# A planner's cost model is rewritten: dependent neighbours, transfers, measured times, and four buffers for decoded tiles

## The chip, the cores and the metric

The kernel runs on one core of one Trainium2 chip. The metric is the device time of one execution in microseconds (us). The core has a matrix engine (TensorE, PE in the profile), a vector engine (VectorE, DVE), an activation engine (ScalarE, ACT), a general engine (GpSimd, POOL) and SyncE (SP), which here issues the transfers. Each engine runs its own queue in order; semaphores tie the queues together.

## The reference

Three parts are computed in sequence, for a batch of 4, all in float32.

- **Attention with decay.** 8 heads, 768 tokens, head size 48. With f = sigmoid(f_logit), a state of 48 x 48 per head is updated at every token, `state = f * state + outer(k, v)`, and `y = q @ state`. The heads are then joined to x of 768 x 384.
- **Block 1, a gated MLP.** `h = gelu_tanh(x @ w_in)` with 1024 columns, cut into u and v of 512. v is normalised over its 512 columns (mean, variance, eps 1e-6), multiplied by `g_ln`, mixed over tokens, `v_s = w_sg @ v_n + b_sg`, and `x = x + (u * v_s) @ w_out`.
- **Block 2, a mixing in the complex plane.** `theta = x @ w_theta`; `y = w_tok_r @ (x cos theta) + w_tok_i @ (x sin theta)`; `u = x + y`; the result is `u + relu(u @ w_ch)`.

The weights w_in, w_out, w_theta, w_ch, w_tok_r and w_tok_i come as float64, seen as pairs of 32-bit words; the kernel turns them into float32 itself (a "decode"). w_sg comes as float32.

## The kernel before, in words

**Matmuls in three parts.** Each float32 operand is split into a high part (a cast on ScalarE, `split` line 792, `xsplit` line 802, `load_split` line 446) and a low part (a subtraction on VectorE, lines 793, 803, 447). `mm3` (line 775) then multiplies high by high, high by low and low by high: lines 783, 784 and 785.

**Attention** (`half`, `unit`). The sequence is taken in two halves of 384 tokens, the heads in four pairs. A half loads the logits and q, k, v, makes decays with a scan on VectorE (line 562 for batch 0, line 578 else), and their logarithms and inverses on ScalarE (Ln and Exp, lines 583 and 584). A unit, one pair of one half, then runs on TensorE: transposes of k (628), updates (640) and scores (649), products inside a chunk (704) and products carried from earlier chunks (722). Between these ScalarE copies the transposed k (kt, 632), VectorE masks the scores (661) and sums the states (677 to 686) with ScalarE's scaling (691), and ScalarE copies y out (733). y goes by transfer into x's layout (`xst<-y`, 756). There are 32 units: 8 for each batch.

**Block 1** (`block1`): the v half of x @ w_in with gelu and statistics for six token tiles, p2 (u), p3 (token mixing; its PSUM is read on line 846), p4 (w_out). For batch b it is interleaved with the attention of batch b + 1. Per token tile, the sum of v comes from the gelu's accumulator (958), GpSimd multiplies it by -1/512 (963), ScalarE adds it (964) and squares with an accumulator (967); VectorE and GpSimd make the inverse root (974, 979).

**Block 2** (`block2`): theta with sine and cosine (888 to 898), p6 (token mixing with two weight matrices), p7 (w_ch). It runs for the last batch first and then for batches 0 to 2, whose x waits in DRAM.

**Weights.** The 24 tiles of w_tok_r and w_tok_i are decoded in the background (`decode`): load into `raw`, one ScalarE and four VectorE instructions into `dt` (432 to 436), the two parts into `wt`, a write to DRAM (`scratch<-wt`, 483). There is one `wt` buffer (`N_W = 1`). w_theta and w_ch are decoded into one buffer `wmid` of three tiles and written to DRAM in one transfer each (`channel_weights`). Streams read the tiles back (`st<-scratch`, 493) into five buffers.

**The order of the work.** The whole program is described as operations with an engine, a duration, the buffers read and written and a due time. `Plan.schedule` then simulates the engines in Python when the kernel is built and writes each engine's queue in the order that the simulation gives; nothing is reordered on the chip. It first moves due times back from successors. Then, for each engine, it takes the operations that could start within `LOOK` of the earliest one, and of these the one with the earliest due time, ScalarE's table switches being charged `SWITCH = 2.0`. Two operations on the same engine follow one another at once, by `lat`. A transfer is given an issue time, a rate and a landing time. PE's clock is modelled too, and while the plan is below 100 us, filler matmuls (line 1029) are put into TensorE's gaps.

Of the kernel before, what the change touches and what calls it, by code (L numbers as in the profile page):

```python
# [8 lines left out]
F32 = mybir.dt.float32  # L9
F32R = mybir.dt.float32r  # L10
# [38 lines left out]
WARM_GAP = 0.3  # L49
N_W = 1  # L50
N_DT = 3
# [59 lines left out]
class Op:  # L111
    __slots__ = ("eng", "dur", "fn", "deps", "succ", "left", "vt", "n", "start", "end", "need", "table", "dma", "est", "cols")


class Plan:
# [57 lines left out]
    def schedule(self):  # L173
        for o in reversed(self.ops):
            cost = LAT[o.eng] + o.dur + ((1.6 + o.dma / 360e3) * DMA_SLACK if o.dma else 0.0)
            for d in o.succ:
                o.vt = min(o.vt, d.vt - cost)
        free = {e: 0.0 for e in LAT}
        ticks = {}
        cand = {e: [] for e in LAT}  # L180
        table, dev, dge = None, 0.0, 0.0
        for o in self.ops:
# [49 lines left out]
        while todo:  # L232
            pick = None
            for e, c in cand.items():
                best = None
                ready = []
                for o in c:
                    t = o.est
                    if o.need:
                        u = slot_time(o)  # L240
                        if u is None:
                            continue
                        t = max(t, u)
# [80 lines left out]
def body(tc, ctx, att, qkv, flog, w_in, g_ln, w_sgT, b_sg, w_out, w_theta, w_rT, w_iT, w_ch, out):  # L324
# [42 lines left out]
    def make_state(attention):  # L367
# [6 lines left out]
        g.ar = [Slots(main, f"ar{i}_", 1) for i in range(3)]  # L374
        g.wmid = Slots(main, "wmid", 1)
        g.stat = Slots(main, "stat", 2)
# [23 lines left out]
    def dma(pl, eng, nbytes, fn, r=(), w=(), wp=(), vt=None):  # L400
        pl.op(eng, {"SP": 0.47, "ACT": 0.66, "POOL": 1.05}[eng], fn, r, w, wp, dma=nbytes, vt=vt)

# [6 lines left out]
    def a1(n):  # L409
        return 0.1 + n * 0.00081  # L410
# [50 lines left out]
    def channel_weights(pl, g, i, vt):  # L461

        w = pl.buf(g.wmid, [P, 2, NK, DM], F32R)
        src, scale = ((w_theta, 1.0 / (2.0 * math.pi)), (w_ch, None))[i]
        for k in range(NK):
            load_split(
                pl, g, w, lambda k=k: (w.t[:, 0, k], w.t[:, 1, k]), src[k * P : (k + 1) * P], vt + k * 2.0, scale, background=True
            )
        dma(pl, "SP", P * 9216, lambda: nc.sync.dma_start(scratch2[i], w.t.bitcast(F32)), [w], [g.scr2[i]], vt=vt + 6.0)

    def channel_load(pl, g, i, vt, place=None):

        w = pl.buf(g.wmid, [P, 2, NK, DM], F32R) if place is None else Buf(t=win[:, :, :, place * DM : (place + 1) * DM])
        old = [] if place is None else [x for xs_ in g.win for x in xs_]
        dma(pl, "SP", P * 9216, lambda: nc.sync.dma_start(w.t.bitcast(F32), scratch2[i]), [g.scr2[i]], [w, *old], vt=vt)
        return w
# [112 lines left out]
    def unit(pl, g, b, hf, p, f, fb, seed, sb, be, bb, t, parts, xst, carry):  # L589
# [42 lines left out]
        pl.op("ACT", a1(TH), lambda: nc.scalar.mul(kt.t, ps.t[:, 0, :TH], -1.0), r=[ps], w=[kt])  # L632
        nu = 2 * NC2 - hf
# [20 lines left out]
        here = Buf()  # L654
        pl.op("PE", 1.15, scores, r=[kb, qb, vb, kt], w=[ps, here])
        if before:
# [17 lines left out]
        def state(c):  # L674
            (s0, b0), (s1, b1) = S[c], S[c + 1]
            if hf == 0 and c == 0:
                pl.op("DVE", 0.2, lambda: V.tensor_copy(s1(), U(0)), r=[ps], w=[b1])
            elif c % 2 or c == 0:
                b1 = fulls[c // 2] if c % 2 else b1
                s1 = (lambda: st.t[:, 2 * NC2 + c // 2]) if c % 2 else s1  # L680
                pl.op("DVE", 0.16, lambda: V.tensor_add(s1(), s0(), U(c)), r=[ps, b0], w=[b1])  # L681
            else:
                be_ = be[:, c // 2 - 1 : c // 2]
                pl.op(
                    "DVE", 0.19,
                    lambda: V.scalar_tensor_tensor(s1(), st.t[:, 2 * NC2 + c // 2 - 1], be_, U(c), ALU.mult, ALU.add), r=[ps, fulls[c // 2 - 1], bb], w=[b1],
# [39 lines left out]

        carry["last"] = [qb, *(S[c][1] for c in late)], [ps], 0.15 * len(late), carried

        def output():
            y = pl.buf(g.y, [P, NC2, 2, HP])  # L730
            pl.op(
                "ACT", a1(TH),
                lambda: nc.scalar.copy(
# [36 lines left out]
    def moe(pl, g, xst, get, wmid, out_b, pace, first=False):  # L770
# [48 lines left out]
        def p2(hf):  # L819
            us = []  # L820
            for d in range(ND):
# [5 lines left out]
                u = pl.buf(g.u, [P, TH])  # L827
                pl.op("ACT", a1(TH), lambda u=u, ps=ps: A(u.t, ps.t[:, :TH], AF.Gelu_apprx_tanh), [ps], [u], table="G")  # L828
                us.append(u)
# [38 lines left out]
        def theta(hf, w):  # L868
            for i in range(NC2):
# [13 lines left out]

                pl.op("PE", 0.33, transposes, r=xst[hf].parts, w=[xps])
                pl.vt += 0.4 * pace
# [47 lines left out]
        def block1(before, resplit, keep=None):  # L933
# [10 lines left out]
            for s in range(NS):  # L944
# [7 lines left out]
                for k in range(NK):  # L952
# [8 lines left out]

                m = lambda s=s: stat.t[:, 0, s : s + 1]
                pl.op("POOL", 0.15, lambda m=m: nc.gpsimd.tensor_scalar(m(), m(), -1.0 / DH, None, ALU.mult), w=[sm[s]])
                pl.op("ACT", a1(DH), lambda m=m, vt=vt: A(vt.t, vt.t, AF.Identity, bias=m()), [sm[s]], [vt])  # L964
                pl.op(
                    "ACT", a1(DH) + 0.1,
                    lambda vt=vt, s=s: A(junk, vt.t, AF.Square, accum_out=stat.t[:, 1, s : s + 1]), [vt], [sv[s]],  # L967
                )
                vts.append(vt)
                if s % 3 == 2:  # L970
                    gs = slice(s - 2, s + 1)
                    pl.op(
                        "DVE", 0.07,
                        lambda gs=gs: V.tensor_scalar(stat.t[:, 2, gs], stat.t[:, 1, gs], 1.0 / DH, 1e-6, ALU.mult, ALU.add),
                        sv[gs], sr[gs],
# [56 lines left out]
    with tc.manual_schedule():  # L1032
        def between():
# [8 lines left out]
            pl.vt = U_AT  # L1042
            dma(pl, "SP", 2048, lambda: nc.sync.dma_start(gcol, g_ln), wp=[g.const])
            dma(pl, "SP", P * 3072, lambda: nc.sync.dma_start(bbc, b_sg.partition_broadcast(P)), wp=[g.const])
# [61 lines left out]
    def general():  # L1106
# [48 lines left out]
        with tc.For_i(0, B, 1) as b:  # L1155
# [4 lines left out]
            for hf in range(2):  # L1160
# [23 lines left out]
            one, two = moe(  # L1184
                pl, g, xin, lambda pl, i: stream(pl, g, i, 0.0), lambda pl, i: channel_load(pl, g, i, 0.0),
                out[bass.ds(b, 1)].squeeze(0), 1.0,
# [51 lines left out]
```

## Time and profile before

| | |
|---|---|
| median of 3 runs | 666.63 us (664.45 to 668.9) |
| profiled execution | span 668.6 us; highest of the three times 668.9 us |
| TensorE busy (matmul) | 616.4 us, 92% |
| TensorE weight loads | 568.9 us, 85% |
| VectorE busy | 445.6 us, 67% |
| ScalarE busy | 357.9 us, 54% |
| GpSimd busy | 30.0 us, 4% |
| transfers | 131.49 MB, mean 197 GB/s |

Busy times are the union of an engine's instructions over the span; a matmul's record is longer than the step to the next one, since they are pipelined. The page lists groups of instructions by source line and the chain of work that ended last. Block 1 of the last batch ends near 420 us; the rest of the span is block 2.

### The profile page before, as it was taken

The page shows a single profiled execution, that of the slowest core. Times are in us where ns is not written, and L with a number is a line of the kernel's source. Part 1 is how long each engine was busy: PE and PEld are TensorE (multiplying, and loading weights), DVE is VectorE, ACT ScalarE, POOL GpSimd, SP SyncE. Part 2 cuts the span into 40 slices and gives each one's busy share as a digit, 9 for nine tenths or more (in the row PEclk, how much of TensorE's full clock was granted, in tenths as well). Part 3 has the DMA queues.
Part 4 walks back from the last instruction along what each step waited for, and adds up shares of the span by engine and source line. Part 5 has one row for each costly group of instructions (what it writes and reads, how often), then busy time and mean ns, then how long its engine had stood idle before and what let it go on. Part 6 is the DMA issues. An engine that isn't in the chain of part 4 may idle for free.

```text
span 668.6 us, 14971 instructions
## 1 busy us (share of the span) xinstructions
PE 616.4 (92%) x5963; PEld 568.9 (85%) x5963; DVE 445.6 (67%) x1029; ACT 357.9 (54%) x754; POOL 30.0 (4%) x56
## 2 busy tenths in 40 slices
PE   9788699799999989899989999899999999999996
PEld 8677478687788877698878999899989999998996
DVE  6999689988879987758767488731581175148203
ACT  6759695667695557774337543730390065029200
POOL 2001010000200001200001000000000000000000
PEclk9999899899999999799989999999999999999999
DMA  8531846297456885444776678268628844860762
GB/s 327 207 93 52 308 159 212 90 311 247 161 156 221 296 286 178 137 134 151 227 251 221 213 278 295 73 193 254 203 78 279 249 161 145 255 214 25 250 198 76
DMA packets 54383, 131.49 MB, mean 197 GB/s; under 512 B 6816, under 2 KB 21664, under 8 KB 54048
## 3 DMA queue, kind: packets, MB, share of 16 engines
q1 hardware_dynamic: 54304, 130.45, 59.2%
q8 instruction: 49, 0.80, 0.5%
q14 instruction: 30, 0.25, 0.1%
HBM read 100.93 MB, written 24.77 MB: 188 GB/s over the span
## 4 chain that ended last, share of the span: by engine, by line
PE 45%; DVE 21%; ACT 17%; DMA 12%; issue 3%; POOL 1%; SPq 0%; POOLq 0%; DVEq 0%; ACTq 0%
PE mm L783 14%; PE mm L785 14%; PE mm L784 14%; DMA scratch<-wt 4%; DMA xst<-y 2%; DMA qkv<-in_qkv 2%; ACT junk L967 2%; ACT tmp L964 2%; DVE tmp L846 2%; DMA f<-in_flog 1%; ACT tmp L958 1%; DMA st<-scratch 1%; DVE s L681 1%; ACT ar L792 1%; DMA raw<-in_w_iT 1%
## 5 line engine op out<-in xcount | busy, mean ns | idle before, releaser
L783 PE MATMUL mm<-st,ar 128*128 128x384 f32 x480 | 164.3, 342 | 0.3 <-ACT u L828 0.3
L785 PE MATMUL mm<-st,ar 128*128 128x384 f32 x480 | 160.7, 335 | 0.0
L784 PE MATMUL mm<-st,ar 128*128 128x384 f32 x480 | 160.6, 334 | 0.0
L802 ACT CAST x<-xst 128x384 fp32r<-128x384 f32 x72 | 36.8, 513 | 165.9 <-DVE xst L807 125.8
L807 DVE TENSOR_TENSOR xst<-xst,mm 128x384 f32<-128x384 f32 x48 | 25.6, 551 | 112.4 <-PE mm L785 112.3
L783 PEld LDWEIGHTS mm<-st,ar 128*128 128x128 f32 x480 | 90.1, 188 | 3.2 <-ACT u L828 0.6
L784 PEld LDWEIGHTS mm<-st,ar 128*128 128x128 f32 x480 | 90.2, 188 | 0.2
L785 PEld LDWEIGHTS mm<-st,ar 128*128 128x128 f32 x480 | 90.1, 188 | 0.0
L783 PE MATMUL mm<-win,x 128*128 128x512 f32 (+1 forms) x144 | 56.9, 395 | 11.6 <-ACT x L802 5.3
L783 PE MATMUL mm<-x,win 128*128 128x384 f32 x168 | 59.0, 351 | 1.0 <-DVE tmp L846 1.0
L785 PE MATMUL mm<-x,win 128*128 128x384 f32 x168 | 57.0, 339 | 0.8 <-DVE win L447 0.8
L784 PE MATMUL mm<-x,win 128*128 128x384 f32 x168 | 56.8, 338 | 0.0
L785 PE MATMUL mm<-win,x 128*128 128x512 f32 (+1 forms) x144 | 54.1, 376 | 1.1 <-DVE x L803 1.1
L784 PE MATMUL mm<-win,x 128*128 128x512 f32 (+1 forms) x144 | 54.0, 375 | 0.1
L792 ACT CAST ar<-tmp 128x384 fp32r<-128x384 f32 x80 | 37.6, 509 | 17.3 <-DVE tmp L851 16.5
L803 DVE TENSOR_TENSOR x<-xst,x 128x384 fp32r<-128x384 f32 x72 | 37.7, 552 | 8.1 <-ACT x L802 6.1
L783 PEld LDWEIGHTS mm<-win,x 128*128 128x128 f32 x144 | 27.9, 194 | 17.8 <-DVE tmp L846 6.7
L793 DVE TENSOR_TENSOR ar<-tmp,ar 128x384 fp32r<-128x384 f32 x80 | 41.0, 552 | 1.4 <-ACT ar L792 0.8
L783 PE MATMUL mm<-ar,wout 128*128 128x384 f32 x96 | 34.8, 363 | 1.8 <-DVE tmp L898 1.8
L783 PEld LDWEIGHTS mm<-x,win 128*128 128x128 f32 x168 | 31.9, 190 | 2.4 <-DVE tmp L846 1.3
L785 PEld LDWEIGHTS mm<-x,win 128*128 128x128 f32 x168 | 32.0, 190 | 1.1 <-DVE win L447 1.1
L784 PE MATMUL mm<-ar,wout 128*128 128x384 f32 x96 | 32.9, 342 | 0.0
(139 smaller groups left out, 1159.1 us busy)
## 6 DMA issues: line engine op xcount, KB each, us to landing
st<-scratch SPq DMA_DIRECT2D x132, 384.0 KB, 3.8
qkv<-in_qkv SPq DMA_DIRECT2D x28, 536.0 KB, 6.2
scratch<-wt SPq DMA_DIRECT2D x24, 384.0 KB, 3.5
f<-in_flog SPq DMA_DIRECT2D x6, 768.0 KB, 5.2
scratch<-st SPq DMA_DIRECT2D x12, 384.0 KB, 6.1
raw<-in_w_rT SPq DMA_DIRECT2D x12, 384.0 KB, 4.0
raw<-in_w_iT SPq DMA_DIRECT2D x12, 384.0 KB, 4.3
out<-xst SPq DMA_DIRECT2D x24, 192.0 KB, 1.9
```

Of the source, the lines that this page charges most:

```text
L681: pl.op("DVE", 0.16, lambda: V.tensor_add(s1(), s0(), U(c)), r=[ps, b0], w=[b1])
L783: nc.tensor.matmul(o, h0, h1, start=start, stop=False)
L784: nc.tensor.matmul(o, h0, l1, start=False, stop=False)
L785: nc.tensor.matmul(o, l0, h1, start=False, stop=stop)
L792: pl.op("ACT", a1(n), lambda: nc.scalar.copy(tiles()[0], src.t[:, :n]), [src], [hi])
L793: pl.op("DVE", v1(n), lambda: V.tensor_sub(tiles()[1], src.t[:, :n], tiles()[0].bitcast(F32)), [src, hi], [lo])
L802: pl.op("ACT", a1(TH), lambda: nc.scalar.copy(X[hf][:, 0, k], T()), [src], [hi])
L803: pl.op("DVE", v1(TH), lambda: V.tensor_sub(X[hf][:, 1, k], T(), X[hf][:, 0, k].bitcast(F32)), [src, hi], [lo])
L807: pl.op("DVE", v1(TH), lambda: V.tensor_add(T(), T(), ps.t[:, :TH]), [ps], [xst[hf].parts[k]])
L846: lambda t=t, d=d: V.scalar_tensor_tensor(t.t[:, :TH], pss[d].t[:, :TH], gcol[:, d : d + 1], bbc[:, hf * TH : (hf + 1) * TH], ALU.mult, AL ...
L964: pl.op("ACT", a1(DH), lambda m=m, vt=vt: A(vt.t, vt.t, AF.Identity, bias=m()), [sm[s]], [vt])
L967: lambda vt=vt, s=s: A(junk, vt.t, AF.Square, accum_out=stat.t[:, 1, s : s + 1]), [vt], [sv[s]],
```

## The change: what it does

- The planner's same-engine step between an operation and one that reads or overwrites its result costs `DRAIN` (0.12 us on VectorE, 0.14 on ScalarE, 0.05 on GpSimd); before it cost nothing.
- `LOOK` goes from 0.05 to 0.15, and an operation that would start later than the earliest candidate is charged 15 times the delay on its due time (`STALL`).
- Transfers: issue 0.43 us, 1.2 us from issue to the data path, 335e3 bytes per us in place of 360e3, 0.6 us to land. A transfer is not planned while more than 2.5 us of others are queued (`BACKLOG`), nor while eight are in flight.
- Durations of the attention's operations, of the ScalarE copies and of the transposes in theta are set anew.
- `N_W` goes from 1 to 4; `wmid` goes, w_theta and w_ch use `wt` buffers and three transfers each.
- GpSimd's scaling of the mean (963) goes: ScalarE's Identity now computes sum - 512 v, the square is scaled by 1/512, the variance is formed with the factor 512 and an eps scaled alike, and `gcol` is negated once on VectorE.

```diff
-N_W = 1
+N_W = 4
-LOOK = 0.05
+LOOK = 0.15
+STALL = 15.0
+BACKLOG = 2.5
+ISSUED = 1.2
+LANDED = 0.6
+RATE = 335e3
+DRAIN = {"PE": 0.0, "DVE": 0.12, "ACT": 0.14, "POOL": 0.05, "SP": 0.0}
...
+        o.made = frozenset(deps)
...
-            cost = LAT[o.eng] + o.dur + ((1.6 + o.dma / 360e3) * DMA_SLACK if o.dma else 0.0)
+            cost = LAT[o.eng] + o.dur + ((ISSUED + LANDED + o.dma / RATE) * DMA_SLACK if o.dma else 0.0)
...
+                    if o.dma and e != "POOL":
+                        t = max(t, dev - BACKLOG, lands[-8] if len(lands) >= 8 else 0.0)
...
-                    vt = o.vt + (SWITCH if self.loads(o, table) else 0.0)
+                    vt = o.vt + (SWITCH if self.loads(o, table) else 0.0) + (t - t0) * STALL
...
-            if o.dma and o.eng != "POOL":
-                dge = t = max(t, dge)
-                dge += dur
...
-                dev = max(dev, o.end + 0.65) + o.dma / 360e3
-                o.end = dev + 0.95
+                dev = max(dev, o.start + ISSUED) + o.dma / RATE
+                o.end = dev + LANDED
+                if o.eng != "POOL":
+                    lands.append(o.end)
...
-                d.est = max(d.est, o.end + (0.0 if o.dma else lat(o.eng, d.eng)))
+                wait = 0.0 if o.dma else lat(o.eng, d.eng) if o.eng != d.eng else DRAIN[o.eng] if o in d.made else 0.0
+                d.est = max(d.est, o.end + wait)
...
-        w = pl.buf(g.wmid, [P, 2, NK, DM], F32R)
...
+            w = pl.buf(g.w32, [P, 2, DM], F32R)
...
-        dma(pl, "SP", P * 9216, lambda: nc.sync.dma_start(scratch2[i], w.t.bitcast(F32)), [w], [g.scr2[i]], vt=vt + 6.0)
+            dma(
+                pl, "SP", P * 3072, lambda w=w, k=k: nc.sync.dma_start(scratch2[i][:, :, k], w.t.bitcast(F32)), [w],
+                wp=[g.scr2[i]], vt=vt + 2.0 + k * 2.0,
+            )
...
-        pl.op("PE", 0.36, transposes, r=[kb, *carry.get("sums", ())], w=[ps])
+        pl.op("PE", 0.25, transposes, r=[kb, *carry.get("sums", ())], w=[ps])
...
-        pl.op("PE", 1.15, scores, r=[kb, qb, vb, kt], w=[ps, here])
+        pl.op("PE", 0.25 + 0.1 * nu, scores, r=[kb, qb, vb, kt], w=[ps, here])
...
-        pl.op("PE", 0.55, inner, r=[vb, am], w=[ps, sums])
+        pl.op("PE", 0.5, inner, r=[vb, am], w=[ps, sums])
...
-        carry["last"] = [qb, *(S[c][1] for c in late)], [ps], 0.15 * len(late), carried
+        carry["last"] = [qb, *(S[c][1] for c in late)], [ps], 0.134 * len(late), carried
...
-                pl.op("POOL", 0.15, lambda m=m: nc.gpsimd.tensor_scalar(m(), m(), -1.0 / DH, None, ALU.mult), w=[sm[s]])
-                pl.op("ACT", a1(DH), lambda m=m, vt=vt: A(vt.t, vt.t, AF.Identity, bias=m()), [sm[s]], [vt])
                 pl.op(
                     "ACT", a1(DH) + 0.1,
-                    lambda vt=vt, s=s: A(junk, vt.t, AF.Square, accum_out=stat.t[:, 1, s : s + 1]), [vt], [sv[s]],
+                    lambda vt=vt, s=s: A(vt.t, vt.t, AF.Identity, bias=stat.t[:, 0, s : s + 1], scale=-float(DH)), [sm[s]], [vt],
+                )
+                pl.op(
+                    "ACT", a1(DH) + 0.1,
+                    lambda vt=vt, s=s: A(junk, vt.t, AF.Square, scale=1.0 / DH, accum_out=stat.t[:, 1, s : s + 1]), [vt], [sv[s]],
                 )
...
+            pl.op("DVE", 0.07, lambda: nc.vector.tensor_scalar(gcol, gcol, -1.0, None, ALU.mult), w=[g.const])
```

## Rows read from the trace of the kernel before

**Rows 1.** Busy time by stage: length, then each engine's busy us (and instructions), clock, transfers.
```profile
0.00:54.00 54.00, 46.59 (x834) 41.41 (x835) 46.12 (x144) 35.38 (x84) 5.88 (x18) 1.00 0.59 204
54.00:156.00 102.00, 84.86 (x1179) 72.90 (x1179) 86.03 (x206) 74.91 (x150) 7.15 (x11) 0.95 0.59 198
...
480.00:540.00 60.00, 59.18 (x344) 57.96 (x343) 26.83 (x54) 22.58 (x48) 0.00 (x0) 1.00 0.62 198
```

**Rows 2.** TensorE's waits after 54 us: us in total, times, longest.
```profile
PE mm L783 <- DVE tmp L846: 5.9, 5, 2.9
PE at L640 <- ACT kt L632: 5.8, 6, 2.2
PE mm L783 <- ACT x L802: 5.3, 1, 5.3
PE at L704 <- DVE s L686: 4.9, 5, 1.4
PE at L628 <- ACT y L733: 3.5, 2, 3.2
PE mm L882 <- DVE tmp L898: 2.9, 7, 0.4
PE at L704 <- DVE s L681: 2.1, 4, 0.9
```

**Rows 3.** Chain of waits that ended last, near 72 us: start, us, what.
```profile
71.80 7.75 DMA xst<-y
```

**Rows 4.** Timeline, 117 to 125 us: start, us, instruction.
```profile
118.19 0.76 PE L722 MATMUL at<-qkv,s 48*48 48x64 f32 x20
...
122.31 1.25 ACT L828 ACTIVATE u<-mm 128x384 f32<-128x384 f32 x3
...
123.44 0.49 ACT L733 COPY y<-at 128x384 f32<-128x384 f32 x1
```

**Rows 5.** Timeline, 271 to 275 us.
```profile
271.24 3.10 POOL L963 TENSOR_SCALAR stat<-stat 128x1 f32<-128x1 f32 x1 [6.92 <-ACT tmp L958]
...
274.37 0.73 ACT L964 ACTIVATE tmp<-tmp,stat 128x512 f32<-128x512 f32 x1 [2.99 <-POOL stat L963]
```

**Rows 6.** Timeline, 339 to 347 us.
```profile
343.82 0.36 DVE L434 TENSOR_SCALAR dt<-dt 128x384 int32<-128x384 int32 x1
...
344.68 0.62 DVE L846 SCALAR_TENSOR_TENSOR tmp<-mm,gcol,bbc 128x384 f32<-128x384 f32 x1
...
345.36 0.50 PE L783 MATMUL mm<-win,x 128*128 128x512 f32 x1 [2.85 <-DVE tmp L846]
```

**Rows 7.** Busy time in the stretches of lower granted clock (columns as in Rows 1).
```profile
79.48:86.30 6.82, 4.60 (x10) 2.67 (x10) 6.05 (x10) 6.59 (x7) 0.00 (x0) 0.50 0.80 305
...
123.85:127.27 3.42, 3.28 (x12) 3.29 (x13) 2.37 (x7) 1.96 (x7) 0.00 (x0) 0.50 0.41 108
...
277.45:284.28 6.83, 6.83 (x102) 6.13 (x103) 4.02 (x12) 5.88 (x14) 0.88 (x1) 0.50 0.43 117
...
345.72:349.13 3.41, 3.41 (x10) 2.64 (x9) 3.38 (x8) 2.01 (x4) 0.00 (x0) 0.50 0.19 74
```

**Rows 8.** TensorE's timeline, 286 to 288 us: updates and scores, then the next matmul.
```profile
286.69 0.56 PE L640 MATMUL at<-qkv,kt 64*64 64x48 f32 x24
...
287.55 0.45 PE L783 MATMUL mm<-x,win 128*128 128x384 f32 x1
```

**Rows 9.** All waits over the span, one row: us in total, times, longest.
```profile
ACT wt L446 <- DMA scratch<-wt: 15.8, 11, 4.7
```

**Rows 10.** VectorE's timeline in the head, 22 to 34 us.
```profile
26.80 0.55 DVE L600 TENSOR_TENSOR ar<-ar 128x384 f32<-128x384 f32 x1
27.39 0.56 DVE L602 SCALAR_TENSOR_TENSOR ar<-ar,ar 128x384 f32<-128x384 f32 x1
27.86 0.16 DVE L557 TENSOR_SCALAR ar<-ar 128x3 f32<-128x3 f32 x1
```

**Rows 11.** Groups of instructions by line: count, busy us, mean ns of one.
```profile
L312 ACT ACT_TABLE_LOAD x17 | 21.8, 1283 | 1.1 <-PEq L1230 0.8
```

More of the change, by code (lines that the diff above doesn't have):

```diff
@@ L111 @@
 class Op:
-    __slots__ = ("eng", "dur", "fn", "deps", "succ", "left", "vt", "n", "start", "end", "need", "table", "dma", "est", "cols")
+    __slots__ = ("eng", "dur", "fn", "deps", "succ", "left", "vt", "n", "start", "end", "need", "table", "dma", "est", "cols", "made")
 class Plan:
@@ L180, in schedule @@
         cand = {e: [] for e in LAT}
-        table, dev, dge = None, 0.0, 0.0
+        table, dev, lands = None, 0.0, []
         for o in self.ops:
@@ L374, in make_state @@
         g.ar = [Slots(main, f"ar{i}_", 1) for i in range(3)]
-        g.wmid = Slots(main, "wmid", 1)
         g.stat = Slots(main, "stat", 2)
@@ L400, in dma @@
     def dma(pl, eng, nbytes, fn, r=(), w=(), wp=(), vt=None):
-        pl.op(eng, {"SP": 0.47, "ACT": 0.66, "POOL": 1.05}[eng], fn, r, w, wp, dma=nbytes, vt=vt)
+        pl.op(eng, {"SP": 0.43, "ACT": 0.66, "POOL": 1.05}[eng], fn, r, w, wp, dma=nbytes, vt=vt)
     def v2(n):
@@ L461, in channel_weights, with channel_load @@
     def channel_weights(pl, g, i, vt):
-        w = pl.buf(g.wmid, [P, 2, NK, DM], F32R)
         src, scale = ((w_theta, 1.0 / (2.0 * math.pi)), (w_ch, None))[i]
         for k in range(NK):
+            w = pl.buf(g.w32, [P, 2, DM], F32R)
             load_split(
-                pl, g, w, lambda k=k: (w.t[:, 0, k], w.t[:, 1, k]), src[k * P : (k + 1) * P], vt + k * 2.0, scale, background=True
+                pl, g, w, lambda w=w: (w.t[:, 0], w.t[:, 1]), src[k * P : (k + 1) * P], vt + k * 2.0, scale, background=True
             )
-        dma(pl, "SP", P * 9216, lambda: nc.sync.dma_start(scratch2[i], w.t.bitcast(F32)), [w], [g.scr2[i]], vt=vt + 6.0)
-    def channel_load(pl, g, i, vt, place=None):
-        w = pl.buf(g.wmid, [P, 2, NK, DM], F32R) if place is None else Buf(t=win[:, :, :, place * DM : (place + 1) * DM])
-        old = [] if place is None else [x for xs_ in g.win for x in xs_]
+            dma(
+                pl, "SP", P * 3072, lambda w=w, k=k: nc.sync.dma_start(scratch2[i][:, :, k], w.t.bitcast(F32)), [w],
+                wp=[g.scr2[i]], vt=vt + 2.0 + k * 2.0,
+            )
+    def channel_load(pl, g, i, vt, place):
+        w = Buf(t=win[:, :, :, place * DM : (place + 1) * DM])
+        old = [x for xs_ in g.win for x in xs_]
         dma(pl, "SP", P * 9216, lambda: nc.sync.dma_start(w.t.bitcast(F32), scratch2[i]), [g.scr2[i]], [w, *old], vt=vt)
@@ L628, in transposes @@
                 nc.tensor.transpose(ps.t[:, 0, c], K()[:, c], ident)
-        pl.op("PE", 0.36, transposes, r=[kb, *carry.get("sums", ())], w=[ps])
+        pl.op("PE", 0.25, transposes, r=[kb, *carry.get("sums", ())], w=[ps])
         kt = pl.buf(g.kt, [P, TH])
-        pl.op("ACT", a1(TH), lambda: nc.scalar.mul(kt.t, ps.t[:, 0, :TH], -1.0), r=[ps], w=[kt])
+        pl.op("ACT", a1(TH) - 0.04, lambda: nc.scalar.mul(kt.t, ps.t[:, 0, :TH], -1.0), r=[ps], w=[kt])
         nu = 2 * NC2 - hf
@@ L676, in state @@
             if hf == 0 and c == 0:
-                pl.op("DVE", 0.2, lambda: V.tensor_copy(s1(), U(0)), r=[ps], w=[b1])
+                pl.op("DVE", 0.115, lambda: V.tensor_copy(s1(), U(0)), r=[ps], w=[b1])
             elif c % 2 or c == 0:
@@ L680, in state @@
                 s1 = (lambda: st.t[:, 2 * NC2 + c // 2]) if c % 2 else s1
-                pl.op("DVE", 0.16, lambda: V.tensor_add(s1(), s0(), U(c)), r=[ps, b0], w=[b1])
+                pl.op("DVE", 0.115, lambda: V.tensor_add(s1(), s0(), U(c)), r=[ps, b0], w=[b1])
             else:
@@ L684, in state @@
                 pl.op(
-                    "DVE", 0.19,
+                    "DVE", 0.12,
                     lambda: V.scalar_tensor_tensor(s1(), st.t[:, 2 * NC2 + c // 2 - 1], be_, U(c), ALU.mult, ALU.add), r=[ps, fulls[c // 2 - 1], bb], w=[b1],
@@ L731, in output @@
             pl.op(
-                "ACT", a1(TH),
+                "ACT", a1(TH) - 0.04,
                 lambda: nc.scalar.copy(
@@ L827, in p2 @@
                 u = pl.buf(g.u, [P, TH])
-                pl.op("ACT", a1(TH), lambda u=u, ps=ps: A(u.t, ps.t[:, :TH], AF.Gelu_apprx_tanh), [ps], [u], table="G")
+                pl.op("ACT", a1(TH) - 0.04, lambda u=u, ps=ps: A(u.t, ps.t[:, :TH], AF.Gelu_apprx_tanh), [ps], [u], table="G")
                 us.append(u)
@@ L882, in transposes @@
                         nc.tensor.transpose(xps.t[:, k * P : (k + 1) * P], xst[hf].t[:, k, tt], ident)
-                pl.op("PE", 0.33, transposes, r=xst[hf].parts, w=[xps])
+                pl.op("PE", 0.39, transposes, r=xst[hf].parts, w=[xps])
                 pl.vt += 0.4 * pace
@@ L973, in block1 @@
                         "DVE", 0.07,
-                        lambda gs=gs: V.tensor_scalar(stat.t[:, 2, gs], stat.t[:, 1, gs], 1.0 / DH, 1e-6, ALU.mult, ALU.add),
+                        lambda gs=gs: V.tensor_scalar(stat.t[:, 2, gs], stat.t[:, 1, gs], float(DH), 1e-6 * DH * DH, ALU.mult, ALU.add),
                         sv[gs], sr[gs],
@@ L1042, in between @@
             pl.vt = U_AT
-            dma(pl, "SP", 2048, lambda: nc.sync.dma_start(gcol, g_ln), wp=[g.const])
+            dma(pl, "SP", 2048, lambda: nc.sync.dma_start(gcol, g_ln), w=[g.const])
+            pl.op("DVE", 0.07, lambda: nc.vector.tensor_scalar(gcol, gcol, -1.0, None, ALU.mult), w=[g.const])
             dma(pl, "SP", P * 3072, lambda: nc.sync.dma_start(bbc, b_sg.partition_broadcast(P)), wp=[g.const])
@@ L1184, in general @@
             one, two = moe(
-                pl, g, xin, lambda pl, i: stream(pl, g, i, 0.0), lambda pl, i: channel_load(pl, g, i, 0.0),
+                pl, g, xin, lambda pl, i: stream(pl, g, i, 0.0), lambda pl, i: channel_load(pl, g, i, 0.0, i),
                 out[bass.ds(b, 1)].squeeze(0), 1.0,
```

1 line of the change is left out of this document (removed).

## The prediction

> **What bounds the kernel now.** I read first the busy time by stage [rows 1]. In block 2 (480 to 540 us) TensorE is busy 59.18 of 60 us: nothing that reorders work can give much there. In the first 54 us VectorE is busy 46.12 us and TensorE mostly runs fillers: the head is VectorE's. Between them lies block 1 with the attention of the next batch woven in; from 54 to 156 us TensorE is busy 84.86 of 102 us, VectorE 86.03, ScalarE 74.91. No engine is full, so the time goes in waits between them.
>
> Next I asked what TensorE waited for after 54 us [rows 2]. I sort the seven rows by what waits. At the attention's own matmuls: 5.8 + 4.9 + 3.5 + 2.1 = 16.3 us. At dense matmuls (lines 783 to 785): 5.9 + 5.3 = 11.2 us. At block 2's transposes: 2.9 us. The longest single waits in these rows are 5.3, 3.2, 2.9 and 2.2 us, together 13.6 of the first 27.5, so I looked at each.
> - **74 us, 5.3.** The split of x waits for y's copy into xst, which took 7.75 us to land [rows 3]; it had been issued behind loads that nobody needed yet.
> - **121 us, 3.2.** TensorE's carried matmuls end at 118.95, yet the copy of y that frees their PSUM runs on ScalarE at 123.44, behind three gelus among others [rows 4]; the next unit's transposes wait 3.2 us for it. ScalarE's order was wrong, not its speed.
> - **275 us, 2.2.** One negated mean on GpSimd took 3.10 us, ScalarE idled 2.99 us for it [rows 5], and the kt copy behind it came late.
> - **342 us, 2.9.** The PSUM bank that the next matmul needs is freed by a VectorE instruction that runs at 344.68, behind other work, instructions of a background decode (line 434) among it; TensorE waits 2.85 us [rows 6].
>
> Then the clock [rows 7]. Four stretches, 20.5 us in all, ran at 0.50, that is 1.2 GHz. Each begins at or just after the end of one of these four waits, with TensorE nearly idle before it. In them TensorE was busy 4.60 + 3.28 + 6.83 + 3.41 = 18.1 us; at 2.4 GHz the same work takes half, so 9.1 us were lost.
>
> **The change, part by part.** Hardly an instruction is removed. What changes is the order in which the planner writes each engine's queue, because its costs change; so each part is priced by the waits that a wrong order left.
>
> *Measured times.* The old cost of updates and scores together is 1.15 us; the trace shows 0.86 from the first of them to the next matmul [rows 8]. The new cost is 0.25 + 0.1 x 6 = 0.85. With transposes, inner and carried parts also cut, the old planner believed one attention unit to be about 0.6 us longer on TensorE than the new one does (2.96 against 2.40 with six carried pieces). A planner that thinks TensorE late puts other work ahead of what TensorE needs next: that is the picture at 121 us. Bounds for the 16.3 us at attention matmuls: none or all of it goes. I take 8.2, half, because about half of all waits looked at lies in the few long ones, which are plainly errors of order, while waits of about 1 us can be true latency. New errors of order can cost as well; that is a rival.
>
> *Transfers and four buffers.* The planner now holds a transfer back while 2.5 us of others are queued, so a late y goes ahead of background loads; and a decoded tile no longer waits until the one before it has been written out. That wait cost ScalarE 15.8 us of idle time, eleven times [rows 9], and holds VectorE up behind it, as near 342 us. The two 1152 KB writes of w_theta and w_ch become six of 384 KB: four issues more on SP, the same bytes; I cost them at nothing, as SP mostly waits for other engines, and without that cover each would delay the transfer behind it by one issue. For the dense waits of 11.2 us the bounds are again 0 and all; I take half, 5.6.
>
> *Bubbles.* On VectorE, line 602 reads what line 600 wrote and starts 0.59 us after it; line 557, which does not read line 602's result, starts 0.47 us after that [rows 10]. So a dependent neighbour costs 0.12 us more, the new cost for it. I count six such places in one of the eight units of the head, 0.7 us a unit, 5.6 us in all: an estimate. Bounds 0 and 5.6; I take half, 2.8, as the head is one chain of which only the next unit's work can fill in. The Trainium skill, VectorE: DVE Perf Modes, section "The DRAIN you can't avoid", says that after a VectorE op the next one "does not start until the 8-stage pipe empties", adds that one which is not held starts earlier, and the page's advice is to cut the number of ops. Taken as it stands for every neighbour, order gains nothing, this term is 0 and the sum 2.8 us longer. The trace does not bear that out for neighbours that do not depend on each other.
>
> *The mean on ScalarE.* 24 small GpSimd instructions and two hops each go. ScalarE's count is the same: one Identity, now with the negated length as scale. Its new neighbour, reading the accumulator, may stall up to 0.14 us by the planner's figure, 24 times, with the Square and the next gelu queued behind it; I cost that at nothing because other ScalarE work can stand between, and at 3.4 us on ScalarE without it. The gain is the 2.2 us wait already counted. One tiny multiply of gcol on VectorE waits for gcol's load, long before its first reader.
>
> *Block 2.* Its 2.9 us are chains through sine, product and split; a quarter goes, 0.7. *Clock.* If the four long waits go, their stretches go, but new ones may open; of 9.1 I take half, 4.5.
>
> **Sum:** 8.2 + 5.6 + 2.8 + 0.7 + 4.5 = 21.8 us off. All rows come from an execution of 668.6 us span (the highest of the three times, 668.9, is nearest to it), about 2 us above the median of 666.63. From the span it gives 646.8; against the median, 644.8. I forecast **645 us**. With nothing gained it is 667; with all terms whole (16.3 + 11.2 + 5.6 + 2.9 + 9.1 = 45.1), 621.5.
>
> **Rivals.**
> - *Nearly all goes.* If order alone made the waits, three quarters and more of 45.1 go: 34 to 45 us, about 627. For it: three of the four long waits are plainly order. Against: VectorE and ScalarE are busy 84% and 73% in the worst stage [rows 1]. 13%.
> - *The waits move.* A greedy planner trades one 1 us wait for another; only the mean's 2.2 us and its half-clock stretch (6.83 / 2 = 3.4) are sure. 666.6 - 5.6 = 661, within 1%. For it: the shares of busy time just named, and the many short waits. 20%.
> - *Slower: table loads.* The new rule charges 15 x 0.14 = 2.1 for a bubble on ScalarE, and 2.0 for a table switch. Between Ln and the Exp that reads it, a gelu that is ready now looks cheaper than the bubble, and costs a load there and one back. Now there are 17 loads of 1.283 us [rows 11]. Six Ln-Exp pairs in batches 1 to 3 make up to 12 more: 15.4 us on ScalarE, in the stages where TensorE waits for it. If they fall there, the waits above stay too: 666.6 + 15.4 = 682. It decides when the loads on the path cost more than the 21.8 us saved, or when fewer reopen the waits. Against: due times must favour the gelu by almost nothing less than the Exp's. 16%. The Trainium skill, ScalarE: Activation LUTs, section "What ACT_TABLE_LOAD costs", gives about 2.66 us for a switch with its drain; by that these twelve would be 31.9 us and the time 698.5. The rows that I read bear out its 1283 ns for the load itself.
>
> My forecast has the remaining 51%, with a range of its own of 633 to 656.
>
> **The numbers.** 1% is 6.7 us, about what a measurement of this kernel can tell from no change: faster is below 660, slower above 673. Faster: 51 + 13 + 4 of the second rival = 68%. Same: its other 16%. Slower: 16%. The range from 620 to 668 takes in the forecast with the bounds of its terms, most of the first rival and nearly all of the second; it leaves out the slower one.
>
> **What would show it.** Right: after 54 us TensorE's waits for kt, y and the state sums fall to about half of 16.3 us, no single one over 2 us; the wait of the cast into wt for its write-out goes; fewer than four stretches at 0.50; the first dense matmuls of block 1 start two to three us earlier; block 2 stays near 60 us a batch. Wrong: more than 17 table loads with gelu between Ln and Exp; as many long waits at other places; or a head that is longer than before.

## The result: 1.15% faster, a third of what was forecast

The changed kernel takes **658.74 us** (median of four runs, 657.3 to 661.66) against 665.67 for the kernel before (four runs, 664.45 to 668.9): a ratio of 0.9885 [0.9843, 0.9927]. The forecast was 645, in a range of 620 to 668: the direction held and the time lies in the range, but 6.9 us were saved where 21.8 were summed.

The two profiled spans lie further apart than the medians: 668.6 and 656.2 us, 12.4 us. The runs of the changed kernel last 1.8 us longer than their spans, so the execution profiled before took about 670.4 (an estimate), 4.7 above its median and above all its timed runs; the one profiled after took 658.03, 0.7 below. 12.4 - 4.7 - 0.7 = 7.0, the 6.9 of the medians. What follows explains the 12.4.

The page of the changed kernel; first the busy time of the engines:

```profile
span 656.2 us, 15080 instructions
...
PE 616.3 (94%) x6033; PEld 572.8 (87%) x6033; DVE 440.7 (67%) x1030; ACT 353.9 (54%) x752; POOL 20.1 (3%) x32
```

TensorE's waits after 54 us (columns as in [rows 2]); all of them are shown:

```profile
PE mm L794 <- DVE tmp L857: 4.9, 5, 1.3
PE mm L794 <- ACT win L454: 4.6, 1, 4.6
PE at L651 <- ACT kt L643: 3.2, 4, 1.9
PE mm L893 <- DVE tmp L909: 2.6, 7, 0.4
PE mm L794 <- DMA st<-scratch: 2.3, 1, 2.3
PE at L715 <- DVE s L697: 2.2, 2, 1.2
PE mm L794 <- issue: 2.1, 1, 2.1
PE mm L794 <- ACT u L839: 1.9, 1, 1.9
PE mm L794 <- DVE tmp L909: 1.7, 1, 1.7
PE mm L794 <- DVE tmp L902: 1.5, 2, 1.3
PE mm L794 <- DVE held L1116: 1.4, 1, 1.4
PE mm L795 <- DVE st L455: 0.6, 1, 0.6
PE at L660 <- DVE qkv L626: 0.4, 1, 0.4
```

Lines have moved down by 8 to 12: 794 to 796 are the dense matmuls (783 to 785 in [rows 2]), 651 and 715 the attention's (640, 704). Sort them as the prediction did. The attention's four rows, 16.3 us before, are now 3.2 + 2.2 = 5.4; the row for y and one of the two for the state sums are gone. The two dense rows that the prediction counted fell from 11.2 to 4.9. But the dense matmuls have new rows: all dense rows together are now 21.0 us, and were 16.3. All rows of this view sum to 38.4 before and 29.4 after. In the seven rows that the prediction read, 17.5 of 30.4 us went (to 5.4 + 4.9 + 2.6 = 12.9); in all other rows 8.0 became 16.5, 8.5 us more.

The clock: outside the last microseconds two stretches at 1.2 GHz are left of the four in [rows 7] (columns as in [rows 1]), 10.2 us long:

```profile
57.99:64.81 6.82, 4.32 (x13) 4.32 (x14) 4.88 (x18) 6.79 (x19) 0.86 (x1) 0.50 0.12 40
119.43:122.84 3.41, 3.35 (x10) 3.35 (x11) 2.29 (x7) 2.15 (x7) 0.00 (x0) 0.50 0.75 246
```

Half of the busy time in them is 3.8 us, against 9.1 before: 5.3 saved. 9.0 of waits and 5.3 of clock make 14.3, more than the 12.4 us of the spans. The 1.9 between them are fillers: a gap that the planner closes with one (before 100 us of its plan) is busy time and no longer a wait in the view above. Filler matmuls from 54 to 100 us, before and after (length, TensorE's matmul and weight-load us, clock, transfers):

```profile
54.00:100.00 46.00, 2.54 (x18) 2.16 (x18) 0.93 0.51 176
```
```profile
54.00:100.00 46.00, 4.44 (x36) 4.23 (x36) 0.93 0.59 199
```

**Where it was given back.** The stages, after, and one row of before that answers to the last but one:

```profile
0.00:54.00 54.00, 50.00 (x838) 45.49 (x839) 45.51 (x143) 33.41 (x80) 5.89 (x18) 1.00 0.58 202
54.00:156.00 102.00, 89.68 (x1254) 78.50 (x1253) 83.82 (x206) 75.86 (x153) 4.74 (x5) 0.95 0.61 202
...
380.00:480.00 100.00, 91.55 (x524) 87.96 (x523) 57.80 (x122) 42.01 (x89) 0.00 (x0) 1.00 0.64 213
```
Before:
```profile
380.00:480.00 100.00, 96.06 (x552) 94.11 (x552) 56.27 (x116) 37.34 (x77) 0.00 (x0) 1.00 0.67 223
```

From 54 to 156 us TensorE is 4.8 us busier than in [rows 1], 1.9 of it with fillers; from 380 to 480 us it is 4.5 us less busy than before. Counted by dense matmuls (the nth of each kernel, at the changed kernel's time), TensorE is 2 us ahead of before at 150 us, 14 at 270 and 18.8 at 360, and only 12.4 from 441 us to the end. So 6.4 us are lost again around the start of block 2, where the prediction looked for no loss. Two places of it, the first on all engines (start us, us, instruction), the second on TensorE alone:

```profile
394.99 0.36 DVE L441 TENSOR_SCALAR dt<-dt 128x384 f32<-128x384 f32 x1 [1.59 <-ACT dt L440]
395.38 0.36 DVE L442 TENSOR_SCALAR dt<-dt 128x384 int32<-128x384 int32 x1
395.78 0.56 DVE L443 SCALAR_TENSOR_TENSOR dt<-raw,dt 128x384 int32<-128x384 int32 x1
396.25 2.19 DVE L857 SCALAR_TENSOR_TENSOR tmp<-mm,gcol,bbc 128x384 f32<-128x384 f32 x4
...
396.97 0.41 PE L794 MATMUL mm<-win,x 128*128 128x384 f32 x1 [2.06 <-issue]
```
```profile
438.55 0.41 PE L794 MATMUL mm<-st,ar 128*128 128x384 f32 x1 [2.31 <-DMA st<-scratch]
```

At 394 us the instruction that frees PSUM (857) stands behind three of a background decode that had itself waited for ScalarE, as at 342 us before [rows 6]. At 436 us a load of weights comes late. That background decode is w_ch's, the last tensor decoded. When SP wrote it out (count, then ns, then first and last start), before and after:

```profile
L469 SPq DMA_DIRECT2D scratch<-wmid x2: 364/414/464, 226.1 to 410.3; - x2
```
```profile
L478 SPq DMA_DIRECT2D scratch<-wt x6: 525/569/616, 200.9 to 425.6; - x6
```

The line writes w_theta first and w_ch last. TensorE is some 14 us ahead of before there, and w_ch's last third goes out 15 us later than the whole of it did.

**The table loads** did not come; there are two fewer than in [rows 11]:

```profile
L321 ACT ACT_TABLE_LOAD x15 | 19.2, 1283 | 1.1 <-PEq L1243 0.8
```

### The profile page after: what moved, and what is told of

Same layout as the page of the kernel before. It is cut to its first block, busy times and chain, and to the rows that moved or that the text cites. A ratio compares the mean times of both kernels' runs of the same rounds, so it can differ in the third digit from the quotient of the medians.

```text
span 656.2 us, 15080 instructions
## 1 busy us (share of the span) xinstructions
PE 616.3 (94%) x6033; PEld 572.8 (87%) x6033; DVE 440.7 (67%) x1030; ACT 353.9 (54%) x752; POOL 20.1 (3%) x32
## 4 chain that ended last, share of the span: by engine, by line
PE 57%; ACT 13%; DMA 13%; DVE 12%; issue 3%; SPq 1%; POOL 0%; ACTq 0%; DVEq 0%; POOLq 0%
PE mm L794 16%; PE mm L796 15%; PE mm L795 15%; DMA xst<-y 3%; PE mm L1041 3%; DMA raw<-in_w_rT 2%; ACT ar L803 2%; DMA raw<-in_w_iT 2%; PE at L733 2%; PE at L651 2%; DMA st<-scratch 2%; DMA scratch<-st 1%; PE at L715 1%; PE at L660 1%; DVE dt L443 1%
## 5 line engine op out<-in xcount | busy, mean ns | idle before, releaser
L794 PE MATMUL mm<-win,x 128*128 128x512 f32 (+1 forms) x144 | 56.0, 389 | 8.5 <-DVE tmp L857 3.6
L796 PE MATMUL mm<-win,x 128*128 128x512 f32 (+1 forms) x144 | 52.7, 366 | 0.0
L795 PE MATMUL mm<-win,x 128*128 128x512 f32 (+1 forms) x144 | 52.6, 365 | 0.0
L803 ACT CAST ar<-tmp 128x384 fp32r<-128x384 f32 x80 | 37.7, 509 | 10.7 <-DVE tmp L862 10.2
L794 PEld LDWEIGHTS mm<-x,win 128*128 128x128 f32 x168 | 32.2, 192 | 7.1 <-ACT win L454 4.7
L794 PE MATMUL mm<-ar,wout 128*128 128x384 f32 x96 | 34.7, 361 | 3.6 <-ACT u L839 1.9
L1041 PE MATMUL mm<-ident 128*128 128x128 f32 x256 | 34.5, 292 | 1.6 <-POOL ident masks.py:199 1.6
L1041 PEld LDWEIGHTS mm<-ident 128*128 128x128 f32 x256 | 32.4, 205 | 2.2 <-POOL ident masks.py:199 1.6
```

Of the source, the lines that this page charges most:

```text
L794: nc.tensor.matmul(o, h0, h1, start=start, stop=False)
L795: nc.tensor.matmul(o, h0, l1, start=False, stop=False)
L796: nc.tensor.matmul(o, l0, h1, start=False, stop=stop)
L803: pl.op("ACT", a1(n), lambda: nc.scalar.copy(tiles()[0], src.t[:, :n]), [src], [hi])
L1041: nc.tensor.matmul(g.mm.tiles[i][:, :P], ident, ident, start=True, stop=True)
```

## Experiments

Ratios are to the kernel before on the same chip, with 95% intervals. "Measured times" are the attention's, copies' and transposes' durations; "transfers" the new rates with `BACKLOG` and the eight in flight; "bubbles" `DRAIN`, `STALL` and `LOOK`.

### Was the 3.1 us mean an accident?

**e0_before**: the kernel before, profiled again (no edit).

> The kernel before, unchanged, profiled once more. Theory A (the profile that the prediction was summed on held an accident): the one GpSimd mean of 3.10 us at 271 us is not there again, nor the 2.3 us wait of TensorE and the stretch of lower clock behind it, and the span is 662 to 665 us in place of 668.6. Theory B (the long mean belongs to the kernel): it is there again at the same place and the span is 667 us or more.

669.36 us, span 667.6. It came again (start us, us, instruction):

```profile
271.31 3.36 DVE L578 TENSOR_TENSOR_SCAN f<-f,seed 128x1536 f32<-128x1536 f32 x1
...
271.60 3.09 POOL L963 TENSOR_SCALAR stat<-stat 128x1 f32<-128x1 f32 x1 [6.93 <-ACT tmp L958]
...
274.71 0.73 ACT L964 ACTIVATE tmp<-tmp,stat 128x512 f32<-128x512 f32 x1 [2.98 <-POOL stat L963]
```

The GpSimd instruction begins 0.3 us after VectorE's scan and ends with it: it belongs to the kernel's order.

### Which part carries the gain?

**e6_old_times**: the change without the measured times. **e8_times_only**: before with them alone.

```diff
e6 (from after; the other durations likewise)      e8 (from before; the same lines, the other way)
-        pl.op("PE", 0.25 + 0.1 * nu, scores, r=[kb, qb, vb, kt], w=[ps, here])
+        pl.op("PE", 1.15, scores, r=[kb, qb, vb, kt], w=[ps, here])
```

> The changed kernel with the old durations of the attention's operations, of the ScalarE copies and of the transposes in theta. Theory A (the measured times carry the largest part of the gain): 666 to 674 us, with ScalarE's copies of y and kt late again in front of TensorE's transposes and updates. Theory C: no telling, 652 to 674, other places.

> The kernel before with the measured durations alone (attention's operations, ScalarE's copies, the transposes in theta); costs of neighbours, transfers, buffers and mean as before. Theory A (the measured times carry the gain; without them, e6, the ratio was 1.0003): 656 to 661 us, ratio 0.983 to 0.991. Rival E (the times help only together with the rest): 664 to 670 us.

e6: 668.11 us, 1.0003 [0.9969, 1.0036], nothing gained. e8: 657.76, 0.9851 [0.9824, 0.9878], as much as the whole change. e6's waits after 54 us sum to 29.9 us, hardly more than the 29.4 of after, and the attention's four kinds of rows have gone there too, without the measured times:

```profile
PE at L715 <- DVE s L692: 1.9, 2, 1.1
PE at L715 <- DVE s L697: 1.8, 1, 1.8
...
PE at L639 <- ACT y L744: 0.7, 2, 0.4
PE at L651 <- ACT kt L643: 0.6, 1, 0.6
```

That is 5.0 us, where after has 5.4 and before 16.3; the copies of y and kt that were expected to be late are not. What sets e6 apart is the clock. It has six stretches at 1.2 GHz before the end, three of them long (columns as in [rows 1]):

```profile
80.84:87.67 6.83, 5.12 (x14) 3.93 (x15) 5.99 (x13) 6.46 (x10) 0.00 (x0) 0.50 0.59 231
108.15:114.97 6.82, 6.82 (x80) 6.24 (x81) 5.97 (x17) 3.89 (x12) 0.00 (x0) 0.50 0.28 90
125.21:132.04 6.83, 5.97 (x58) 4.89 (x57) 6.67 (x16) 2.91 (x6) 0.00 (x0) 0.50 0.32 85
```

These three alone cost half of 17.9 us, 9.0; all six cost 14.1, 10.2 more than the two of after, and its span is 9.8 longer. e8 has a single stretch, of 3.4 us:

```profile
119.71:123.12 3.41, 3.41 (x51) 3.29 (x48) 3.31 (x9) 2.15 (x6) 0.00 (x0) 0.50 0.29 76
```

e8's waits sum to 23.9 us, 8.9 of them in the attention's four kinds of rows (kt 6.2, the longest 3.3); its fillers from 54 to 100 us take 10.35 us, 7.8 more than before. In e8 the mean is still on GpSimd, and still the long wait is gone: no instruction of that line exceeds 1.28 us (ns: shortest, median, longest), because the new order no longer puts one right behind the start of that scan.

```profile
L963 POOL TENSOR_SCALAR stat<-stat x24: 207/315/1279, 55.2 to 355.7; 128x1 f32<-128x1 f32 x24
```

### The mean

**e1_mean_only**: before with the mean on ScalarE. **e14_times_mean**: the same on e8. **e2_no_mean**: the change without it.

```diff
e1, e14 (e2 the other way)
...
-                pl.op("POOL", 0.15, lambda m=m: nc.gpsimd.tensor_scalar(m(), m(), -1.0 / DH, None, ALU.mult), w=[sm[s]])
-                pl.op("ACT", a1(DH), lambda m=m, vt=vt: A(vt.t, vt.t, AF.Identity, bias=m()), [sm[s]], [vt])
...
+                    lambda vt=vt, s=s: A(vt.t, vt.t, AF.Identity, bias=stat.t[:, 0, s : s + 1], scale=-float(DH)), [sm[s]], [vt],
...
```

> The kernel before with the mean on ScalarE alone, planner and buffers as before. Theory A (the gain comes from the order that the new planner costs give): 663 to 667 us, ratio 0.996 to 1.002 against before. Rival (the gain is the mean that no longer goes through GpSimd): about 659 us, ratio 0.989.

> The kernel before with the measured times (as e8, 657.76 us) and the mean on ScalarE. In e8 the mean goes through GpSimd as before. If the mean alone costs time whatever the order (e1: 1.0113): 662 to 666 us. If it is worth something or nothing once the order is right: 653 to 659 us.

> The changed kernel with the mean back on GpSimd. Theory A (order): 658 to 661 us, ratio to before 0.989 to 0.993. Rival (mean): the gain goes, 664 to 667 us, ratio near 1.

e1: 673.98, 1.0113 [1.008, 1.0145], slower, and outside both expectations. e14: 660.06, 0.9876 [0.9852, 0.9901], between the two that were expected and not to be told from e8. e2: 672.55, 1.0088 [1.0059, 1.0116], also slower and outside both: taking the mean out costs 2% where putting it in alone costs 1%. So it has no price of its own. e2 also has the measured times, so they do not bring the gain in every order. And e2's order has the long mean again: 2.72 us at 278.91, ending with a scan that began 0.65 us before it, and TensorE waits 2.1 us for the kt copy behind it. In e2 there are 21 table loads, and the pattern of the third rival is in its ScalarE timeline: Ln, a load to gelu, gelus, a load back, Exp.

```profile
54.58 0.53 ACT L576 ACTIVATE ar<-ar 128x384 f32<-128x384 f32 x1 [1.16 <-DVE bends L617]
55.12 1.28 ACT L321 ACT_TABLE_LOAD   x1
56.42 0.60 ACT L969 ACTIVATE tmp<-mm 128x512 f32<-128x512 f32 x1
...
59.71 1.28 ACT L321 ACT_TABLE_LOAD   x1
61.00 0.52 ACT L577 ACTIVATE ar<-ar 128x384 f32<-128x384 f32 x1
```

**e10_no_mean_switch4** and **e15_mean_switch4**: e2 and e1 with a dearer table switch.

```diff
-SWITCH = 2.0
+SWITCH = 4.0
```

> The changed kernel with the mean back on GpSimd, as in e2 (672.55 us, 21 table loads), and the charge for a table switch raised from 2.0 to 4.0, which is more than the 2.1 that a bubble on ScalarE is charged. Theory F (e2 was slow because a switch looked cheaper than a bubble, so that a gelu came between a Ln and its Exp): 17 loads or fewer and 657 to 664 us. Rival (e2 was slow for want of the mean): 669 to 674 us.

> The kernel before with the mean on ScalarE (as e1, 673.98 us, 19 table loads) and the charge for a table switch at 4.0 in place of 2.0. Theory F (e1's loss is its Ln that was cut off from its Exp by gelus): 17 loads and 663 to 669 us. Rival (the loss is of the order at large): 670 to 676 us.

e10: 663.6, 0.991 [0.9875, 0.9946], 17 loads. Four loads less are 5.1 us; 9.0 went. TensorE's longest wait in e2, 6.0 us for a gelu on ScalarE, shrank as well, and the low stretches cost 9.8 us where e2's cost 15.3:

```profile
PE mm L794 <- ACT u L839: 8.0, 2, 6.0
```
```profile
PE mm L794 <- ACT u L839: 4.8, 3, 2.8
```

e15: 673.06, 1.0075 [1.0049, 1.0101], 17 loads where e1 has 19, and no faster: loads are not what slows e1. e1's waits from 54 to 156 us sum to 17.5 us (before 16.6, e8 9.5), but the execution profiled is its fastest of six, 669.36, so what slows the others isn't in it. e15's, at 672.99, has five low stretches that cost 11.7 us, against 9.1 and 6.5 in the two profiles of before. Why these orders are bad stays open.

### Buffers, bubbles, transfers

**e3_one_wt**, **e5_no_bubbles**, **e4_old_transfers**, **e11_times_mean_bufs** (e4 and e5 together) are the change with one part undone.

```diff
e3
-N_W = 4
+N_W = 1
e5
-LOOK = 0.15
-STALL = 15.0
-DRAIN = {"PE": 0.0, "DVE": 0.12, "ACT": 0.14, "POOL": 0.05, "SP": 0.0}
+LOOK = 0.05
+STALL = 0.0
+DRAIN = {"PE": 0.0, "DVE": 0.0, "ACT": 0.0, "POOL": 0.0, "SP": 0.0}
e4
...
-                    if o.dma and e != "POOL":
-                        t = max(t, dev - BACKLOG, lands[-8] if len(lands) >= 8 else 0.0)
...
+            if o.dma and o.eng != "POOL":
+                dge = t = max(t, dge)
+                dge += dur
...
-                dev = max(dev, o.start + ISSUED) + o.dma / RATE
-                o.end = dev + LANDED
+                dev = max(dev, o.end + 0.65) + o.dma / 360e3
+                o.end = dev + 0.95
...
```

> The changed kernel with one buffer for decoded tiles. If the four buffers carry part of the gain: 661 to 664 us, with ScalarE waiting for the write-out of the tile before again (15.8 us in the kernel before). If they carry none: 657 to 660 us.

> The changed kernel with dependent neighbours free again, no charge for a later start and the old look-ahead of 0.05. Theory A: 661 to 664 us, with the dependent pairs on VectorE as many as before. Theory C: anything from 652 to 674; more than 15 table loads would tell of the switches.

> The changed kernel with the planner's old model of transfers (no held-back backlog, no eight lanes, old issue, rate and landing times). Theory A (each part of the planner changes the time by its own size, and the transfers were forecast at about a quarter of the gain): 661 to 664 us. Theory C (any change of a planner cost reshuffles the whole order, and the time moves by up to 2% either way whatever the part is for): anything from 652 to 674, and the waits in the trace move to other places.

> The changed kernel with the old transfers and without the costs of dependent neighbours: measured times, the mean on ScalarE and four buffers stay. If the new transfers cost time, as e4 (654.44 us) against the changed kernel (658.74) says, and the neighbours' costs give nothing, as e5 (659.9) says: 651 to 657 us. If the neighbours' costs help once the transfers are the old ones: 658 to 662 us.

e3: 660.75, 0.9909 [0.9874, 0.9944], between the two expected ranges; its interval overlaps that of after widely. With one buffer ScalarE's waits for the write-out are back, longer than in [rows 9], at no cost that can be told:

```profile
ACT wt L454 <- DMA scratch<-wt: 27.1, 15, 4.8
```

e5: 659.9, 0.9905 [0.9873, 0.9937]: the bubbles bring nothing. The wait of 4.6 us for w_in's cast is not among e5's waits; those from 54 to 156 us are 8.4 us (after 12.2), and its time is no better: its fillers from 54 to 100 us take 10.80 us (after 4.44), and a wait that a filler covers is not saved. It has 19 table loads, without any charge for a bubble. e4: **654.44**, 0.9801 [0.9761, 0.9841], the fastest, outside the 661 to 664 us expected of a part with a size of its own: in this order the new transfers cost about 0.8%, with an interval that ends just where that of after begins. e11: 656.94, 0.9839 [0.9813, 0.9866].

### What hands the gain back at block 2?

**e7_wch_early**: w_ch decoded beside the others, not last. **e13_old_transfers_wch**: that on e4. **e12_no_gate**: the change without the two gates (the first two lines of e4's diff).

```diff
e7, e13
+            if i == 14:
+                channel_weights(pl, g, 1, pl.vt + LATE_AT + (i - N_EARLY) * LATE_STEP)
...
-        channel_weights(pl, g, 1, pl.vt + 20.0)
```

> The changed kernel with w_ch decoded after the 14th of the 24 token tiles in place of last. Theory D (about 6 us of what block 1 gained were given back at the start of block 2, because w_ch's decode and its load of 1152 KB now stand in front of p3's last reads and of p6's tiles): the waits at 394 and 436 us (2.3 and 2.6 us) go and the time falls by 3 to 6 us to 653 to 656. Rival (those waits are not w_ch's doing): 658 to 660, the waits stay.

> The changed kernel with the old transfers (as e4, 654.44 us) and w_ch decoded after the 14th tile (as e7, 656.24 us). If both take away the same wait at the start of block 2, nothing is added: 652 to 657 us. If they take away different ones: 648 to 652 us.

> The changed kernel without the two gates on transfers (backlog of 2.5 us, eight in flight); its new issue, rate and landing times stay. Theory G (the gates put w_ch's writes and its load of 1152 KB between p6's tiles, which is what e4 gained by undoing the transfers): the wait at 436 us goes and the time is 652 to 656 us. Rival (the new rates do it): 657 to 661, the wait stays.

e7: 656.24, 0.9853 [0.9815, 0.9891], profiled span 652.6; its interval overlaps that of after, so the trace has to tell. The wait at 436 us is gone; at 394 us the wait for PSUM is gone and TensorE waits 0.8 us for a load of weights. w_ch's last write-out is at 369.7; in e4 it is at 413.7 and the wait at 436 us is gone too:

```profile
L478 SPq DMA_DIRECT2D scratch<-wt x6: 524/588/987, 201.2 to 369.7; - x6
```
```profile
L477 SPq DMA_DIRECT2D scratch<-wt x6: 519/575/610, 154.1 to 413.7; - x6
```

Counted as above, TensorE's lead falls from 18.2 us at 380 us to 16.1 at 441 in e4, from 18.0 to 15.9 in e7, and from 18.6 to 12.4 in after: 2.1 us lost in each, where after loses 6.2. e13: 655.57, 0.9809 [0.9781, 0.9838], as e4: nothing is added, and its lead falls by 2.0 there (16.1 to 14.1), so the two changes take away the same loss. e12: 657.68, 0.9845 [0.9812, 0.9879], but the wait is still there, and longer, so the gates are not its cause:

```profile
PE mm L792 <- DMA st<-scratch: 4.1, 1, 4.1
```

### How much is a mere reshuffle worth?

**e9_look16**: the change with a setting moved by next to nothing.

```diff
-LOOK = 0.15
+LOOK = 0.16
```

> The changed kernel with a look-ahead of 0.16 in place of 0.15: an edit that should mean nothing. Theory A (the parts have sizes of their own): within 0.4% of the changed kernel, 656 to 661 us. Theory C (every edit of a cost draws a new order and with it up to 2% either way): outside that.

661.39, 0.99 [0.9864, 0.9935]: as after, if 0.4 us past the range that was expected. Its waits are of the same kinds (w_in's cast with 4.5 us the longest), and their sum is 27.2 us. One draw is no measure of the spread, but here it is small beside the 1.5% between before and e8.

## Why the forecast was right in direction and wrong in size

**The step that failed** is the sum's: it prices each part by the waits that the old order left, and puts the waits of the new order at nothing (new errors of order are left to a rival). The waits that it priced did go: 17.5 us of them where 14.5 were forecast, and 5.3 of the clock against 4.5, 22.8 in all, with nothing for the bubbles. But TensorE's waits in rows that no term looked at rose by 8.5 us and the fillers by 1.9, and 12.4 were left. Of these, 5.4 are the executions': the profile before lay 4.7 us above its median, where the prediction took 2, and the one after 0.7 below. That this closes to a tenth is luck: e0's execution of the same kernel lost 6.5 us to the low clock, not 9.1.

- **Measured times: the gain came with them, but not by the road forecast.** 8.2 us were forecast, 10.9 of the 16.3 went. e8 has the gain with this part alone, e6 without it has none; yet in e6 the same waits fell by 11.3 and in e8 by 7.4. So these waits go without the measured times, and their going brings no gain by itself: e6 lost it to the low clock. And e2, with the measured times, is slower than before. Why the orders of after and e8 are good is not shown beyond their waits, fillers and low stretches.
- **Transfers and four buffers: the waits counted went, and as many others came.** Forecast 5.6 of 11.2 us gone. The two rows counted did fall by 6.3, but the dense waits as a whole rose by 4.7 us. The buffers' wait of 15.8 us was ScalarE's own and hid nothing that can be told: e3 brings all of it back. The working took long idle time on an engine that was not the bound [rows 9] for a price on the path. The y wait at 74 us, ascribed to transfer order, goes with the measured times: in e8, which has the old transfers, the row for x is 0.8 us, and in e6, which has the new ones, 3.6.
- **Bubbles: 2.8 us forecast, none found.** The first dense matmul of block 1 starts at 46.58 us in both kernels, so the head gave nothing. v's first gelu starts at 54.5 us (54.1 before), and TensorE then waits 4.6 us for w_in's cast, which stands on ScalarE behind those gelus; the first half-clock stretch follows. e5 has neither and is as fast.
- **The mean: its wait was counted as gone, and its replacement at nothing.** The wait went, but whether it is there depends on the order: e8's has lost it with the mean still on GpSimd, e2's has it again. So the 5.6 us "sure" in the second rival were not the mean's alone.
- **Clock: 4.5 forecast, 5.3 found**, or 2.7 if e0 is taken for before: the stretches vary between executions. Half the busy time is also a little too much: at 345 us before, dense matmuls of 512 columns follow each other at 0.43 us in the low stretch and at 0.23 behind it, so 46% is lost. **Block 2: 0.7 forecast, 0.3 found** (2.9 to 2.6).
- **The sum as such.** Terms were taken wait by wait as if independent. The order is drawn anew by each edit: taking one part out of the change moves the ratio by -0.8% to +2.0%, and the parts' effects do not add up to the whole's. The largest loss, 6.4 us at 394 to 441 us, lies where no term looked. The terms also came from an execution that was put 2 us over the median and was 3.7 over the 666.63 taken there, so some of its waits need not be in a typical one.
- **The signs.** Of those of being right all but one came: the attention's waits fell below half with none over 1.9 us, the cast's wait for its write-out went, two low stretches are left, block 2 kept its pace; the earlier start of block 1 did not come. The sign that counts was among those of being wrong, long waits at other places: there were four of over 2 us, there are three (4.6, 2.3 and 2.1). The direction is in part luck: without the mean (e2) the rest of the change is slower than before.
- **Rivals.** "Waits move", at 661, comes nearest to the time, and others did take the place of the waits that went; but what it held sure, the mean's, is not what was gained. The table loads were real but one edit away: in e2, not in the change. Nor do they need the new charge for bubbles: e1 and e5 have 19 without it.

Open: which part of the new transfer costs brings w_ch late (not the gates, e12; and e14, with the old transfers, has 6.9 us of waits at 380 to 445 us as well, e5, with the new, 3.1), why the mean alone makes an order 1.1% worse, and what in a duration makes an order good.

## What to carry to other kernels

Where a planner writes the queues, compare its durations with start-to-start times of the trace first: e8 had all of the gain with that alone, though e2 shows that they do not make every order good. Don't add up waits of the old order: each edit draws a new one, so follow how far the bound engine is ahead along the whole span, and look at what was timed for the old pace (here the last decode in the background). Add fillers to the waits before comparing two waits' sums. Count the table loads of a new order: a dearer switch took four back in e2's and 9.0 us with them, in e1's two and no time.

## What the runs showed of the hardware

A GpSimd instruction on 128 x 1 elements took 3.10 and 3.09 us in two executions where its median is 0.22, each time ending within 0.02 us of a VectorE scan that had begun before it. Other orders put it later into such a scan, and it was shorter by as much: begun 0.65 us into the scan it took 2.72 us (e2), 1.52 us in 1.84 (e2) and 1.83 (e10), 2.09 us in 1.28 (e8), each time ending with the scan. The Trainium skill, SBUF — State Buffer, section "Who interferes with whom", says that a VectorE instruction with two SBUF inputs contends with a GpSimd one that reads SBUF, and that issue order decides who blocks. The traces agree: the scan reads f and seed, took 3.36 us, and began 0.28 us (0.29 the second time) earlier.

A table load costs ScalarE its own 1.28 us here: in e2's rows the gelu behind one starts 1.30 us after the load does, the Exp 1.29.

Between after and e6 the low clock decided more than the waits' sum: they differ by 0.5 us in waits past 54 us and by 9.8 us in span, and e6 has six low stretches, which cost 14.1 us by half of the busy time, where after has two, which cost 3.8.
